# Strassen's seven products for the output matmuls of a fused attention and MLP kernel on Trainium2

## The chip, the cores and the metric

One core of a Trainium2 chip. The metric is the device time of one execution in microseconds (us), the median of several runs. The engines go by the names of the profile: PE is the matmul engine, PEld its weight loads, DVE is VectorE, ACT is ScalarE, POOL is GpSimd, SP is the engine from whose queue every transfer here is issued (SPq). DVE, ACT, POOL and SP each work through their instructions in the order in which the program has them.

## What is computed

The reference, cut to the part that the change touches:

```python
def _moe2_ref(x, w_in, g_ln, w_sg, b_sg, w_out):   # x: 8 batches x 576 x 512
    h = gelu_tanh(x @ w_in)                        # d_ff = 1024
    u, v = (h[..., :512], h[..., 512:])
    v_n = (v - mean(v)) / sqrt(var(v) + 1e-06) * g_ln
    v_s = einsum('ts,bsd->btd', w_sg, v_n) + b_sg[None, :, None]
    gated = u * v_s
    return x + gated @ w_out
```

Before it come a block-wise attention (chunks of 64) and a layer norm with a feed-forward block of width 2048; their result is the x above, called x2 in the kernel.

## The kernel before, in words

Every large matmul is done with each float32 operand split into two float16 halves, hi and lo, and three products: hi·hi, hi·lo, lo·hi. So each 128-row weight tile meets three matmuls.

The rows are 36 tiles of 128. The first part of the program (attention, the first feed-forward block) runs to about 860 us and is not touched, except for one power of two in the scaling of w_out. The second part, from line 1056, handles the rows in four groups g = 0 to 3 of nine tiles; a group is two batches of 576 rows, called halves e = 0 and e = 1 (each four and a half tiles; tile 4 of the group is shared). Per group it runs these stages, in which a name like `v_unit` is a function of the kernel:

- `prepare` / `x2_make` (line 885): gets x2 of the *next* group ready, in five pieces p = 0 to 4. A piece is loaded from DRAM into a buffer `xs` (two transfers from SP, line 903), DVE makes the sums that Strassen's method needs (lines 910 to 912, one set), ACT writes the hi half (line 927), DVE the lo half (line 936), and SP issues two transposing transfers into `xT` (line 925). There are two `xs` buffers, used in turn.
- `v_unit`, `v8_unit`: the v half of x2 @ w_in; eight tiles by Strassen's seven products (`seven`, line 1109; matmuls at line 1215), the ninth plainly (line 1240). Each product of `seven` fills one PSUM bank, and DVE or ACT takes it out; four banks serve seven products, so products 2, 3 and 4 wait until banks of products 1, 5 and 7 are empty. After it come the gelu and the layer norm (`norm`, statistics at lines 1157 and 1158).
- `u_unit`, `u8_unit`: the u half, the same way (lines 1257 and 1278).
- `s_units(g, e)`: the spatial matmul with w_sg (lines 1310 and 1311), the gate u * v_s (DVE line 1321, POOL line 1328, a rest at lines 1340 and 1346), the largest absolute value of the half (ACT line 1329, DVE line 201, then two small matmuls and lines 1358 to 1364), and the split of the gated half into float16 `gh` (ACT line 1373) and `gl` (DVE line 1376).
- `o_unit(g, i)`: the output tile i, gated @ w_out: twelve matmuls of 512 columns (line 1390), one DVE instruction that scales it and adds x2 (line 1398; `xr` is loaded at line 1393 and stored at line 1401).

The order in which these are recorded is at lines 1421 to 1452; in the groups 0 to 2 the output tiles of group g stand among the v units of group g + 1. The order in which each engine gets them is then made by a list scheduler (`Plan.run`, line 93) from the costs and priorities that each `do(...)`, `pe(...)` and `op(...)` names.

Of the kernel before, what the change touches and what calls it, by code (L numbers as in the profile page):

```python
# [132 lines left out]
def fused_kernel(ctx: ExitStack, tc, qkv, w1, w2, g1, w_in, w_out, wsgt, wsgs, g2, b_sg, out):  # L133
# [675 lines left out]
    def halve(nm, n, i, m, q, full, ck):  # L809
# [142 lines left out]
    with tc.manual_schedule():  # L952
# [118 lines left out]
        wouth, woutl = (bW["wout"][:, :, x] for x in (0, 1))  # L1071
# [217 lines left out]
        def s_units(g, e):  # L1289
# [6 lines left out]
            def unit(m):  # L1296
# [27 lines left out]
                if (g, e) == (NG - 1, 1) and m > 1:  # L1324
# [5 lines left out]
                    out=gh[:, m, 640 * e:640 * e + 512].bitcast(BF16), in_=uv, func=AF.Abs, accum_out=gm.t[:, m:m + 1]  # L1330
                ), uk, [f"g{e}{m}", gm])
# [26 lines left out]
            def cols_():  # L1358
                floor(e_, scr)
                top2(e_, inv)  # L1360
                nc.vector.tensor_scalar_mul(sg, inv, 2.0 ** 14)
# [5 lines left out]
            c = slice(576 * e, 576 * e + 576)  # L1367
            uk = [f"u{x}{m}" for m in range(4) for x in ("ax", "yb")[e]] + ["u8"] * e
            n = 1 if (g, e) == (NG - 1, 1) else 2
            for m in range(0, 4, n):  # L1370
                ms = slice(m, m + n)
                gk = [f"g{e}{m + k}" for k in range(n)]
                do("ACT", 60 + 580 * n, lambda ms=ms: nc.scalar.activation(
                    out=gh[:, ms, c], in_=uT[:, ms, c], func=AF.Copy, scale=sg
                ), uk + [f"c5_{e}"], gk, 1800)
                do("DVE", 60 + 600 * n, lambda ms=ms: nc.vector.scalar_tensor_tensor(
                    out=gl[:, ms, c], in0=uT[:, ms, c], scalar=sg, in1=gh[:, ms, c], op0=ALU.mult, op1=ALU.subtract
                ), uk + [f"c5_{e}"], gk, 1800)

        def o_unit(g, i):  # L1380
            (key, ap), = take(1)
            c = slice(i * 128, i * 128 + 128)
            t = g * GT + i
            xr = ring("xr", 4, [P, D])

            def mm(h):
                n = 6 * h
                for k in (2 * h, 2 * h + 1):
                    for x, w in ((gh, wouth), (gh, woutl), (gl, wouth)):
                        nc.tensor.matmul(ap, lhsT=x[:, k, c], rhs=w[:, k], start=(n == 0), stop=(n == 11))  # L1390
                        n += 1

            do("SP", 730, lambda: nc.sync.dma_start(out=xr.t, in_=x2d[t]), [], [xr], lat=2200)
# [4 lines left out]
            do("DVE", 730, lambda: nc.vector.scalar_tensor_tensor(  # L1398
                out=xr.t, in0=ap, scalar=col(cn), in1=xr.t, op0=ALU.mult, op1=ALU.add
            ), [key, cn], [xr], 1000)  # L1400
            do("SP", 730, lambda: nc.sync.dma_start(out=out[t], in_=xr.t), [xr], [], lat=2200)
# [23 lines left out]
        for g in range(NG):  # L1425
            u_unit(g, 0)
            later = prepare(g + 1, (0, 1))
            u_unit(g, 1)
            if g + 1 < NG:
                u8_unit(g)  # L1430
            for fn in later:
                fn()
            s_units(g, 0)
            if g + 1 == NG:
                u8_unit(g)
            for fn in prepare(g + 1, (2, 3)):
# [4 lines left out]
            if g + 1 < NG:  # L1441
                v_unit(g + 1, 0)
                for i in range(4):
                    o_unit(g, i)
                v_unit(g + 1, 2)
                for i in (5, 6, 7, 8, 4):
                    o_unit(g, i)
                v8_unit(g + 1)
            else:
                for i in (0, 1, 2, 3, 5, 6, 7, 8, 4):  # L1450
                    o_unit(g, i)
# [60 lines left out]
```

## Time and profile before

| | |
|---|---|
| median of 3 runs | 1253.74 us (1253.53 to 1254.8) |
| the profiled execution | 1251.7 us, span 1249.9 us |
| busy share of the span | PE 96%, DVE 65%, ACT 45%, POOL 39% |
| mean granted clock of PE | 0.992 |
| chain that ended last, by engine | PE 70%, DVE 14%, DMA 5%, ACT 4%, POOL 3% |

The profile comes from one execution. Its windows view gives the busy time of each engine in a stretch, its chain follows the work that ended last backwards from the end, its waits say whom an engine waited for. Line numbers in it are those of the kernel before; in the changed kernel everything in the second part stands one line lower up to line 1365, and further down after that.

### The profile page before, as it was taken

How to read it: one execution, taken by the hardware profiler on the slowest of the kernel's cores; microseconds unless marked ns; L12 is line 12 of the kernel's file. 1: busy time of each engine (PE TensorE's matmuls, PEld its weight loads, DVE VectorE, ACT ScalarE, POOL GpSimd, SP SyncE). 2: the span in 40 equal slices, each digit the busy share in tenths (PEclk: the TensorE clock that was granted, in tenths of full speed). 3: DMA queues.
4: the chain of work that ended last, by engine and by line, in shares of the span. 5: the costliest groups of instructions: out<-in, count | busy, mean ns of one | idle time of the engine just before them, and what ended most of it. 6: DMA issues, size and time to landing. Idle time of an engine off the chain costs nothing.

```text
span 1249.9 us, 27025 instructions
## 1 busy us (share of the span) xinstructions
PE 1202.5 (96%) x11412; PEld 890.9 (71%) x11412; DVE 816.2 (65%) x1520; ACT 559.4 (45%) x844; POOL 481.7 (39%) x415
## 2 busy tenths in 40 slices
PE   7899999899998999999999999998999999999998
PEld 5688644577887888888888888887557456456453
DVE  6885125987777676656656664675979559547435
ACT  6776402545665533343333334342745534534321
POOL 3562302544486554444444444342522221323220
PEclk8999999989999999999999999999999999999999
DMA  9863002256321221221322120344183283272203
GB/s 316 258 209 89 1 35 76 60 175 176 87 63 58 52 86 52 69 61 52 77 52 69 52 69 19 79 103 123 35 162 109 84 169 102 84 136 66 88 1 118
DMA packets 140377, 117.81 MB, mean 94 GB/s; under 512 B 104928, under 2 KB 113120, under 8 KB 140256
## 3 DMA queue, kind: packets, MB, share of 16 engines
q1 hardware_dynamic: 140256, 116.09, 34.3%
q8 instruction: 89, 1.46, 0.5%
q14 instruction: 32, 0.26, 0.1%
HBM read 72.02 MB, written 18.87 MB: 73 GB/s over the span
## 4 chain that ended last, share of the span: by engine, by line
PE 70%; DVE 14%; DMA 5%; ACT 4%; POOL 3%; issue 3%; SPq 0%; ACTq 0%; DVEq 0%; POOLq 0%
PE bank L639 16%; PE pair L690 9%; PE pb L1390 7%; PE pb L1310 7%; PE bank L690 6%; PE pb L1215 5%; PE bank L535 5%; PE pb L1257 5%; PE pair L556 3%; PE bank L556 2%; DVE arena L661 1%; DVE tf L599 1%; DMA xs<-x2d 1%; PE pair L294 1%; DMA straw<-in_w 1%
## 5 line engine op out<-in xcount | busy, mean ns | idle before, releaser
L639 PE MATMUL bank<-xT,w1h 128*128 128x256 f16 x1792 | 302.9, 274 | 0.4 <-DVE x L568 0.4
L690 PEld LDWEIGHTS <-arena 128*128 128x128 f16 x2352 | 228.3, 98 | 40.9 <-issue 9.4
L639 PE MATMUL bank<-xT,w1l 128*128 128x256 f16 x896 | 245.0, 273 | 0.0
L668 POOL TENSOR_TENSOR arena<-arena 128x896 f16<-128x896 f32 x69 | 132.7, 1924 | 224.4 <-ACT arena L666 224.3
L639 PEld LDWEIGHTS <-w1h 128*128 128x128 f16 x1792 | 173.6, 98 | 23.3 <-issue 1.3
L666 ACT ACTIVATE arena<-arena 128x896 f16<-128x896 f32 x112 | 106.2, 949 | 181.2 <-DVE arena L663 105.9
L661 DVE TENSOR_TENSOR arena<-arena 128x256 f32<-128x256 f32 x112 | 76.8, 686 | 102.3 <-ACT arena L654 102.2
L690 PE MATMUL pair<-w2s,arena 128*128 128x256 f16 x672 | 110.6, 274 | 7.0 <-ACT u L713 5.9
L654 ACT ACTIVATE arena<-bank 128x512 f32<-128x512 f32 x112 | 66.4, 593 | 107.2 <-PE bank L639 102.0
L690 PE MATMUL pair<-w,arena 128*128 128x256 f16 x672 | 111.2, 274 | 2.9 <-DVE arena L668 1.5
L639 PEld LDWEIGHTS <-w1l 128*128 128x128 f16 x896 | 88.0, 98 | 10.4
L690 PE MATMUL bank<-w,arena 128*128 128x256 f16 x672 | 92.4, 274 | 0.0
L1328 POOL TENSOR_TENSOR uT<-uT,vs 128x512 f32<-128x512 f32 x30 | 40.7, 1357 | 132.6 <-DVE vs L1321 123.5
L535 PE MATMUL bank<-xT,w1h 128*128 128x256 f16 x512 | 87.0, 275 | 3.0 <-DMA xT<-hl 2.8
L1310 PE MATMUL pb<-wsg,vh 128*128 128x512 f16 x288 | 88.5, 380 | 0.0
L1390 PE MATMUL pb<-wout,gh 128*128 128x512 f16 x288 | 85.7, 379 | 0.0
L718 POOL TENSOR_TENSOR x<-x,u 128x256 f32<-128x256 f32 (+1 forms) x60 | 65.2, 1116 | 46.5 <-DVE x L708 34.1
L1215 PEld LDWEIGHTS <-x2T 128*128 128x128 f16 x672 | 66.0, 99 | 16.5 <-issue 6.6
L535 PE MATMUL bank<-xT,w1l 128*128 128x256 f16 x256 | 70.4, 275 | 0.0
L668 DVE TENSOR_TENSOR arena<-arena 128x896 f16<-128x896 f32 x43 | 57.3, 1333 | 17.9 <-ACT arena L666 17.8
L535 PEld LDWEIGHTS <-w1h 128*128 128x128 f16 x512 | 49.2, 98 | 13.8 <-DMA xT<-hl 3.1
L662 DVE TENSOR_TENSOR arena<-arena 128x256 f32<-128x256 f32 x112 | 55.5, 496 | 3.8
(252 smaller groups left out, 2322.4 us busy)
## 6 DMA issues: line engine op xcount, KB each, us to landing
straw<-in_w SPq DMA_DIRECT2D x16, 1023.8 KB, 5.6
qkl<-in_qkv SPq DMA_DIRECT2D x26, 512.0 KB, 3.7
x2d<-x SPq DMA_DIRECT2D x36, 256.0 KB, 2.0
xs<-x2d SPq DMA_DIRECT2D x36, 256.0 KB, 3.3
xr<-x2d SPq DMA_DIRECT2D x36, 256.0 KB, 2.9
out<-xr SPq DMA_DIRECT2D x36, 256.0 KB, 2.8
vl<-in_qkv SPq DMA_DIRECT2D x26, 256.0 KB, 2.7
qk<-in_qkv SPq DMA_DIRECT2D x10, 512.0 KB, 6.2
```

The lines of the kernel that those rows point to most:

```text
L535: nc.tensor.matmul(acc, lhsT=w[j][:, k, fc], rhs=xT.t[:, x, k], start=(n == 0), stop=(n == 11))
L556: nc.tensor.matmul(acc[i], lhsT=h[x].t[:, c], rhs=w2t[j][:, f % 2, y], start=(f == 0 and n == 0), stop=(f == NF - 1 and n == 2),)
L639: nc.tensor.matmul(acc[:, y * 256:y * 256 + 256], lhsT=w[j][:, k, fc], rhs=xT.t[:, x, k], start=(n == 0), stop=(n == 11),)
L654: op("ACT", 600, lambda: nc.scalar.activation(out=o.t[:, 0:4].rearrange("p n t -> p (n t)"), in_=acc, func=AF.Relu, scale=0.5), rd=[kb] + ...
L661: nc.vector.tensor_tensor(out=two(6, 8), in0=two(1, 3), in1=two(0, 2), op=ALU.subtract)
L666: op("ACT", 950, lambda: nc.scalar.activation(out=h.t[:, 0], in_=o.t[:, 1:8], func=AF.Copy), rd=[o] + ar, wr=[h], prio=-100)
L668: op(lo[0], lo[1], lambda: lo[2].tensor_tensor(out=h.t[:, 1], in0=o.t[:, 1:8], in1=h.t[:, 0], op=ALU.subtract), rd=[o], wr=[h], prio=-100)
L690: nc.tensor.matmul(acc, lhsT=h.t[:, x, n], rhs=r(y), start=(first and j == 0 and m == 0), stop=(j == 7 and m == 2), skip_group_check=True,)
L718: op("POOL", ns, lambda: nc.gpsimd.tensor_tensor(out=d(), in0=d(), in1=v(), op=ALU.add), rd=u + ["q6", "q5", "q7"], wr=[x], prio=-50)
L1215: nc.tensor.matmul(ap[:, q * 256:q * 256 + 256], lhsT=xT[:, x, a, k, c], rhs=right(b, 1, k, w), start=(first and n == 0), stop=(k == 1 and ...
L1310: nc.tensor.matmul(ap, lhsT=v[:, fc], rhs=w[:, 0:512], start=(n == 0), stop=end)
L1390: nc.tensor.matmul(ap, lhsT=x[:, k, c], rhs=w[:, k], start=(n == 0), stop=(n == 11))
```

## The change

In the groups 0, 1 and 2 the eight tiles that lie in one half or the other are multiplied with w_out by Strassen's seven products, four tiles of a half at a time (`o_pairs(g, e)`); the shared tile gets a unit of its own (`o4_unit`). The last group keeps `o_unit`. To this end

- the left sides of the products are made once per half: four sums on DVE (`sums` in `s_units`, into a new buffer `gs`), and 3840 instead of 2304 columns are split into halves (`split_g`, ACT and DVE), into `gt` and `g4` in place of `gh` and `gl`;
- the right sides are made once, in group 0 (`wout_sums`, twice: ACT, DVE, four DVE subtractions, ACT, POOL);
- a half's products are taken out of PSUM by one ACT copy and six DVE instructions, with three additions on POOL;
- `split_g` of the second half is recorded behind the first half's `o_pairs`;
- the result of the absolute value on ACT goes to a buffer `jk` that nobody reads;
- to make room, the second `xs` buffer is gone; `xr` buffers hold two tiles each.

```diff
-        gh = pb.tile([P, 4, GT * P], F16, name="gh")
+        gt = pb.tile([P, 2, 7, 2, 256], F16, name="gt")
+        g4 = pb.tile([P, 2, 4, P], F16, name="g4")
+        woT = pb.tile([P, 2, 2, 4, 256], F16, name="woT")
+        jk = pb.tile([P, 512], BF16, name="jk")
-        gl = pb.tile([P, 4, GT * P], F16, name="gl")
-        x2p["xs"].append(pb.tile([P, 9, 256], F32, name="xs1"))
...
+            def sums():
+                S = gs.t
+                for o, x, y, f in (
+                    (S[:, 1], A(0, 0), A(1, 0), ALU.subtract), (A(1, 0), A(1, 0), A(1, 1), ALU.add),
+                    (S[:, 0], A(1, 1), S[:, 1], ALU.subtract), (S[:, 2], A(0, 1), S[:, 0], ALU.subtract),
+                ):
+                    nc.vector.tensor_tensor(out=o, in0=x, in1=y, op=f)
+
+            do("DVE", 2700, sums, [], uk + [gs], 1700)
...
+            parts = [
+                (1024, lambda x: D4(x, 0), lambda: U(0), uk, [f"{gk}0"]),
+                (1536, lambda x: G[:, x, 4:7].rearrange("p n k t -> p (n k t)"),
+                 lambda: gs.t.rearrange("p n k t -> p (n k t)"), [gs], [f"{gk}1"]),
+                (1024, lambda x: D4(x, 1), lambda: U(1), uk, [f"{gk}2"]),
+                (256, lambda x: g4[:, x, :, 64 * e:64 * e + 64], lambda: uT[:, :, t0:t0 + 64], vk, [f"g4{e}"]),
+            ]
...
+        def split_g(n, dst, src, rk, wk, e, sg):
+            do("ACT", 60 + n, lambda: nc.scalar.activation(
+                out=dst(0), in_=src(), func=AF.Copy, scale=sg
+            ), rk + [f"c5_{e}"], wk, 1800)
+            do("DVE", 80 + n * 27 // 25, lambda: nc.vector.scalar_tensor_tensor(
+                out=dst(1), in0=src(), scalar=sg, in1=dst(0), op0=ALU.mult, op1=ALU.subtract
+            ), rk + [f"c5_{e}"], wk, 1800)
...
+        def o_pairs(g, e):
...
+            def mm(p, n, first):
+                a, b = SIDE2[p]
+                i = 0
+                for q in range(2):
+                    for k in range(2):
+                        for x, w in TERMS:
+                            nc.tensor.matmul(
+                                ap[n][:, q], lhsT=G[:, x, a, k, q * 128:q * 128 + 128], rhs=ro(b, k, w),
+                                start=(first and i == 0), stop=(k == 1 and x == 1), skip_group_check=True,
+                            )
+                            i += 1
...
+            prod(1, 0, 0)
+            do("ACT", 680, lambda: nc.scalar.activation(out=O(), in_=ap[0], func=AF.Copy, scale=sc),
+               [key[0], f"c5_{e}"], [o1], 1000)
+            prod(6, 1, 1)
+            do("DVE", 750, lambda: nc.vector.scalar_tensor_tensor(
+                out=O(), in0=ap[1], scalar=sc, in1=O(), op0=ALU.mult, op1=ALU.add
+            ), [key[1], f"c5_{e}"], [o1], 1000)
+            for r, c in ((1, 1), (0, 1), (1, 0)):
+                do("POOL", 1520, lambda r=r, c=c: nc.gpsimd.tensor_tensor(out=C(r, c), in0=C(r, c), in1=O(), op=ALU.add),
+                   [o1], [xr[r]], 1000)
+            prod(5, 2, 2)
+            add(2, 1, 1)
+            prod(7, 3, 1)
+            add(3, 1, 1)
+            prod(2, 0, 0)
+            add(0, 0, 0)
+            prod(3, 2, 1)
+            add(2, 0, 1)
+            prod(4, 3, 2)
+            add(3, 1, 0)
...
+            if g == 0:
+                for k in range(2):
+                    wout_sums(k)
...
+            half()
             for fn in prepare(g + 1, (2, 3)):
                 fn()
-            s_units(g, 1)
+            half = s_units(g, 1)
             for fn in prepare(g + 1, (4,)):
                 fn()
...
+            v_unit(g + 1, 0)
+            o_pairs(g, 0)
+            half()
+            v_unit(g + 1, 2)
+            o_pairs(g, 1)
+            o4_unit(g)
+            v8_unit(g + 1)
```

The schedule moves with it, which the following pieces show as the program has it, without times.

First DVE in group 0, where the gate of the second half ends and the v products of the next group come out of PSUM. Before (`vt` is the rest of the spatial product, `o` and `hv` the v products, `xs` the sums for x2, `gm` and `red` the half's maximum, `xr` an output tile):

```order
L1340 SCALAR_TENSOR_TENSOR vt<-pb_10697,c_c_5173,bb 128x64 x4
L1126 SCALAR_TENSOR_TENSOR o_11526<-pb_10696,e2g,o_11526 128x512
L910 TENSOR_TENSOR xs_5485<-xs_5485 128x2x256
L911 TENSOR_TENSOR xs_5485<-xs_5485 128x2x256
L912 TENSOR_TENSOR xs_5485<-xs_5485 128x256
L1346 TENSOR_TENSOR uT<-uT,vt 128x4x64
L201 TENSOR_REDUCE gm<-uT 128x1
L1126 SCALAR_TENSOR_TENSOR hv<-pb_10697,e2g,o_11526 128x2x256
L201 TENSOR_REDUCE red<-gm 128x1
L1126 SCALAR_TENSOR_TENSOR hv<-pb_10694,e2g,hv 128x2x256
```

And in the changed kernel (`gs` are the new sums of the half, the second `o` row belongs to the output products):

```order
L1341 SCALAR_TENSOR_TENSOR vt<-pb_10697,c_c_5173,bb 128x64 x4
L1127 SCALAR_TENSOR_TENSOR o_11554<-pb_10696,e2g,o_11554 128x512
L1471 SCALAR_TENSOR_TENSOR o_11584<-pb_10692,c_c_0_10723,o_11584 128x512
L936 SCALAR_TENSOR_TENSOR hh_5486<-xs_5485,i2g,hh_10714 128x512
L1347 TENSOR_TENSOR uT<-uT,vt 128x4x64
L201 TENSOR_REDUCE gm<-uT 128x1
L1391 TENSOR_TENSOR gs<-uT 128x512
L1391 TENSOR_TENSOR uT<-uT 128x2x256
L1391 TENSOR_TENSOR gs<-uT,gs 128x512 x2
L201 TENSOR_REDUCE red<-gm 128x1
L1127 SCALAR_TENSOR_TENSOR hv<-pb_10697,e2g,o_11554 128x2x256
```

The four sums have come between the gate and the `hv` row that empties bank 10697, and one x2 piece has made place for the short one.

Second the queue of SP in group 0, where the transposes of the next group's x2 begin. Before:

```order
L903 DMA xs_5485<-x2d_84 128x2x256
L903 DMA xs_5485<-x2d_80 128x2x256
L903 DMA xs_10715<-x2d_85 128x2x256
L903 DMA xs_10715<-x2d_81 128x2x256
L925 DMA_TRANSPOSE x2T<-hh_10708 128x14x128
L925 DMA_TRANSPOSE x2T<-hh_10709 128x14x128
```

And in the changed kernel:

```order
L903 DMA xs_5485<-x2d_83 128x2x256
L903 DMA xs_5485<-x2d_79 128x2x256
L925 DMA_TRANSPOSE x2T<-hh_10711 128x14x128
L925 DMA_TRANSPOSE x2T<-hh_10712 128x14x128
L925 DMA_TRANSPOSE x2T<-hh_10713 128x14x128
L925 DMA_TRANSPOSE x2T<-hh_10714 128x14x128
L903 DMA xs_5485<-x2d_84 128x2x256
L903 DMA xs_5485<-x2d_80 128x2x256
L925 DMA_TRANSPOSE x2T<-hh_5486 128x14x128
L903 DMA xs_5485<-x2d_85 128x2x256
```

The loads of the third piece (tiles 84 and 80) and of the fourth (85 and 81) stood ahead of all transposes; now the third stands behind four of them, and the fourth further down.

## Rows read from the trace of the kernel before

**Rows 1.** Whom PE waited for, 860 to 1250 us (total, times, longest).

```profile
PE pb L1215 <- DVE hv L1126: 2.5, 1, 2.5
PE pb L1215 <- DVE x L708: 2.0, 1, 2.0
PE pb L1257 <- DVE uT L1126: 1.5, 2, 1.0
PE pb L1215 <- DVE vt L1340: 0.8, 1, 0.8
```

**Rows 2.** Busy time by stretch; the first row names the columns.

```profile
core 0: us, PE busy (x) PEld busy (x) DVE busy (x) ACT busy (x) POOL busy (x), PEclk, DMA share, GB/s
907.00:943.50 36.50, 36.22 (x289) 20.52 (x289) 27.50 (x40) 15.66 (x24) 9.06 (x8) 1.00 0.78 159
943.50:983.40 39.90, 39.90 (x246) 23.70 (x244) 35.43 (x66) 22.50 (x27) 12.11 (x12) 1.00 0.31 101
983.40:1004.00 20.60, 20.60 (x132) 10.76 (x131) 8.47 (x13) 8.15 (x11) 4.31 (x5) 1.00 0.26 74
1004.00:1038.50 34.50, 34.50 (x285) 19.77 (x283) 22.93 (x34) 14.52 (x22) 9.24 (x7) 1.00 0.82 161
1038.50:1078.60 40.10, 39.24 (x242) 23.32 (x240) 33.46 (x65) 19.69 (x26) 9.03 (x12) 1.00 0.31 99
...
1100.00:1132.50 32.50, 32.50 (x269) 18.46 (x268) 20.37 (x35) 11.43 (x22) 11.27 (x8) 1.00 0.66 121
1132.50:1172.90 40.40, 40.40 (x250) 24.13 (x249) 24.25 (x50) 18.32 (x24) 13.17 (x12) 1.00 0.28 85
```

**Rows 3.** The chain that ended last: start us, us, what, instructions.

```profile
938.30 5.24 PE pb L1215 x48
...
958.66 9.17 PE pb L1215 x84
967.83 12.95 PE pb L1390 x60
```

**Rows 4.** Groups of DVE, by form, 860 to 1250 us (busy us, mean ns, idle before).

```profile
L936 DVE SCALAR_TENSOR_TENSOR hh<-xs,i2g,hh 128x1792 f16<-128x1792 f32 x12 | 28.3, 2360 | 13.4 <-DMA x2T<-hh 11.5 <-ACT hh L927 1.9
...
L1398 DVE SCALAR_TENSOR_TENSOR xr<-pb,c_c,xr 128x512 f32<-128x512 f32 x32 | 23.7, 747 | 13.2 <-PE pb L1390 13.2
...
L912 DVE TENSOR_TENSOR xs<-xs 128x256 f32<-128x256 f32 x12 | 5.0, 416 | 0.0
...
L1325 DVE TENSOR_TENSOR uT<-uT,vs 128x512 f32<-128x512 f32 x2 | 1.4, 686 | 0.0
```

**Rows 5.** DVE in order of time, around the end of group 0's spatial stage.

```profile
939.85 2.74 DVE L1376 SCALAR_TENSOR_TENSOR gl<-uT,c_sg,gh 128x1152 f16<-128x1152 f32 x2
942.51 0.74 DVE L1321 SCALAR_TENSOR_TENSOR vs<-pb,c_c,bb 128x512 f32<-128x512 f32 x1
943.17 0.84 DVE L1340 SCALAR_TENSOR_TENSOR vt<-pb,c_c,bb 128x64 f32<-128x64 f32 x4
```

**Rows 6.** Groups of ACT and of POOL, by form, 860 to 1250 us.

```profile
L1373 ACT ACTIVATE gh<-uT,c_sg 128x1152 f16<-128x1152 f32 x14 | 16.8, 1244 | 2.5 <-DVE c_sg L1361 2.5
...
L1328 POOL TENSOR_TENSOR uT<-uT,vs 128x512 f32<-128x512 f32 x30 | 40.7, 1357 | 132.6 <-DVE vs L1321 123.5 <-DVE red L201 6.4 <-ACT hh L927 2.7
```

**Rows 7.** POOL in order of time, two places in group 0.

```profile
914.30 1.27 POOL L1328 TENSOR_TENSOR uT<-uT,vs 128x512 f32<-128x512 f32 x1 [8.62 <-DVE vs L1321]
...
966.01 2.20 POOL L1199 TENSOR_TENSOR vl<-hv,vh 128x1024 f16<-128x1024 f32 x1
```

**Rows 8.** DVE at the same two places.

```profile
914.34 3.11 DVE L936 SCALAR_TENSOR_TENSOR hh<-xs,i2g,hh 128x1792 f16<-128x1792 f32 x1
...
965.55 0.68 DVE L910 TENSOR_TENSOR xs<-xs 128x512 f32<-128x512 f32 x1
966.26 2.50 DVE L911 TENSOR_TENSOR xs<-xs 128x512 f32<-128x512 f32 x1
```

**Rows 9.** The queue of SP in order of time, group 0.

```profile
910.06 17.53 SPq L925 DMA_TRANSPOSE x2T<-hh  x8
927.65 1.99 SPq L903 DMA_DIRECT2D xs<-x2d  x3
```

**Rows 10.** The chain that ended last, at the loads of x2 in group 1.

```profile
1019.67 4.37 DMA xs<-x2d
```

More of the change, by code (lines that the diff above doesn't have):

```diff
@@ L1366, in s_units @@
             do("DVE", 700, cols_, [sk], [f"c5_{e}", "c5_m"], 2000)
[L1367 to L1378, printed above, removed]
+            if g == NG - 1:
+                c = slice(576 * e, 576 * e + 576)
+                uk = [f"u{x}{m}" for m in range(4) for x in ("ax", "yb")[e]] + ["u8"] * e
+                n = 1 + (e == 0)
+                for m in range(0, 4, n):
+                    ms = slice(m, m + n)
+                    split_g(
+                        576 * n, lambda x, ms=ms: gl4[:, x, ms, c], lambda ms=ms: uT[:, ms, c], uk,
+                        [f"g{e}{m + k}" for k in range(n)] + [k for k in xk if k[-1] != "4"] * (e == 0), e, sg
+                    )
+                return None
@@ new lines, in halves @@
+            def halves():
+                for part in parts:
+                    split_g(*part, e, sg)
+            return halves
+        def split_g(n, dst, src, rk, wk, e, sg):
[5 more added lines that the diff above has]
+            ), rk + [f"c5_{e}"], wk, 1800)
@@ new lines, in o4_unit, with mm @@
+        def o4_unit(g):
+            (key, ap), = take(1)
+            t = g * GT + 4
+            xr = ring("xr", 4, [P, 2, D])
+            load_x(t, xr, 0)
+            def mm():
+                n = 0
+                for k in range(4):
+                    for x, w in TERMS:
+                        nc.tensor.matmul(ap, lhsT=g4[:, x, k], rhs=wo[:, k, w], start=(n == 0), stop=(n == 11))
+                        n += 1
+            pe(2600, mm, ["g40", "g41"], [key])
+            do("DVE", 730, lambda: nc.vector.scalar_tensor_tensor(
+                out=xr.t[:, 0], in0=ap, scalar=col("c5_m"), in1=xr.t[:, 0], op0=ALU.mult, op1=ALU.add
+            ), [key, "c5_m"], [xr], 1000)
+            store_x(t, xr, 0)
@@ L1397, in o_unit, with wout_sums, sums @@
             cn = "c5_m" if i == 4 else f"c5_{es[0]}"
[L1398 to L1399 removed]
+            do("DVE", 750, lambda: nc.vector.scalar_tensor_tensor(
+                out=xr.t[:, 0], in0=ap, scalar=col(cn), in1=xr.t[:, 0], op0=ALU.mult, op1=ALU.add
             ), [key, cn], [xr], 1000)
[L1401 removed]
+            store_x(g * GT + i, xr, 0)
+        def wout_sums(k):
+            bf, tf = (ring("hv", 4, [P, 2, 512]) for _ in range(2))
+            w = lambda x: wo[:, k:k + 3:2, x]
+            do("ACT", 1080, lambda: nc.scalar.activation(out=bf.t, in_=w(0), func=AF.Copy), [], [bf])
+            do("DVE", 1200, lambda: nc.vector.scalar_tensor_tensor(
+                out=bf.t, in0=w(1), scalar=1.0, in1=bf.t, op0=ALU.mult, op1=ALU.add
+            ), [], [bf])
+            def sums():
+                b = bf.t.rearrange("p k (h e) -> p k h e", h=2)
+                t = tf.t.rearrange("p k (h e) -> p (k h) e", h=2)
+                for o, x, y in (
+                    (t[:, 0], b[:, 0, 1], b[:, 0, 0]), (t[:, 1], b[:, 1, 1], t[:, 0]),
+                    (t[:, 2], b[:, 1, 1], b[:, 0, 1]), (t[:, 3], b[:, 1, 0], t[:, 1]),
+                ):
+                    nc.vector.tensor_tensor(out=o, in0=x, in1=y, op=ALU.subtract)
+            flat = lambda: tf.t.rearrange("p k e -> p (k e)")
+            dst = lambda x: woT[:, k, x].rearrange("p n e -> p (n e)")
+            do("DVE", 1500, sums, [bf], [tf])
+            do("ACT", 1080, lambda: nc.scalar.activation(out=dst(0), in_=flat(), func=AF.Copy), [tf], ["woT"])
+            do("POOL", 2150, lambda: nc.gpsimd.tensor_tensor(out=dst(1), in0=flat(), in1=dst(0), op=ALU.subtract), [tf], ["woT"])
         def prepare(g, ps):
@@ L1425, in fused_kernel @@
         for g in range(NG):
+            more = g + 1 < NG
             u_unit(g, 0)
@@ L1428, in fused_kernel @@
             u_unit(g, 1)
-            if g + 1 < NG:
+            if more:
                 u8_unit(g)
+            if g == 0:
+                for k in range(2):
+                    wout_sums(k)
             for fn in later:
                 fn()
-            s_units(g, 0)
-            if g + 1 == NG:
+            half = s_units(g, 0)
+            if not more:
                 u8_unit(g)
+                s_units(g, 1)
+                for i in (0, 1, 2, 3, 5, 6, 7, 8, 4):
+                    o_unit(g, i)
+                break
+            half()
             for fn in prepare(g + 1, (2, 3)):
                 fn()
-            s_units(g, 1)
+            half = s_units(g, 1)
             for fn in prepare(g + 1, (4,)):
                 fn()
[L1441 to L1451, printed above, removed]
+            v_unit(g + 1, 0)
[5 more added lines that the diff above has]
+            v8_unit(g + 1)
         plan2.run()
```

60 lines of the change are left out of this document (49 added, 11 removed).

## The prediction

> **What bounds the kernel now.** I read the waits of PE first, then the windows, then the chain, then single groups. In the second part of the program (860 us to the end) PE hardly ever waits: four kinds of wait, 6.8 us together, all but 0.8 of them before 908 us [rows 1]. From there it is busy in every stretch at a granted clock of 1.00 [rows 2], and the chain runs through its matmuls [rows 3]. So a column less on PE is time saved, as long as DVE, ACT and POOL deliver in time. DVE is the one to look at: in group 0 it is busy 27.50 of 36.5 us in the spatial stage and 35.43 of 39.9 in the stage of the output and v products; in group 1 it is 22.93 of 34.5 and 33.46 of 40.1, in group 2 20.37 of 32.5 and 24.25 of 40.4. In between, in the u stage, it has much room (8.47 of 20.6) [rows 2].
>
> **What PE saves.** An output tile is twelve matmuls of 512 columns. Sixty of them take 12.95 us: 215.8 ns each, 2.59 us for a tile, 20.7 us for eight tiles [rows 3]. The new product has twelve matmuls of 256 columns; the v products have the same shape, and 84 of them take 9.17 us: 109.2 ns each, 1.31 us for a product [rows 3]. Fourteen products per group are 18.3 us. The saving is 2.4 us per group, 7.1 us over three groups (0.57%). A bound from below is nothing (if the shape did not hold its pace), from above there is none; I take 7.1, since the row is for the same operand types and shape.
>
> The Trainium skill, in "TensorE: Matmul & The Clock Gate" under "Back-to-back issue gap", gives about 131 ns as the sustained spacing of matmuls of 512 columns and 81 for 128 columns. By those figures (98 ns for 256 columns, an estimate between the two) eight tiles would cost 12.6 us before and 16.5 now, and the change would lose about 12 us. The trace disagrees with the rule at 215.8 ns [rows 3], so I give it no chance of its own.
>
> **What DVE gets.** Per half: four sums of 512 columns at 0.686 us [rows 4], 2.74 us. The lo halves go from 2304 to 3840 columns; 1152 columns take 1.37 us where nothing disturbs them (2.74 us for two) [rows 5], so 1536 more are 1.83 us. Six instructions take the products out of PSUM in place of four, at 0.747 us [rows 4]: 1.49 us. Together 6.1 us per half, 12.1 per group. Once, in group 0, the right sides: twice a pass of 1024 columns (1.22 us at the same rate) and four subtractions of 256 columns at 0.416 [rows 4], 5.8 us, of which the order puts half into the u stage of group 0 and half behind it.
>
> **What ACT and POOL get.** ACT: 1536 more columns per half at 1244 ns for 1152, and one copy of about 0.7 us: 2.4 us per half. It is busy 15.66 of 36.5 and 22.50 of 39.9 us [rows 2, 6], so I cost this at nothing; without that cover a half's splits would come 1.7 us later. POOL: three additions per half at 1.27 to 1.36 us [rows 6, 7], 4.0 us; it is busy 13.17 of 40.4 us at most [rows 2], so its own time is covered too. The buffer `jk`, the scaling and the larger `xr` cost nothing that the rows show: the same instructions and bytes go through the same queues.
>
> **But POOL delays DVE.** At 914.34 DVE begins its 1792-column pass just after POOL began a 1.27 us multiplication, and takes 3.11 us; the mean of that form is 2.36. At 966.26 a sum of `xs` begins inside a 2.20 us POOL instruction and takes 2.50 us, where its neighbour took 0.68 [rows 4, 7, 8]. Both read two operands from SBUF; instructions that read PSUM keep their 0.75. The new sums, the splits and the `xs` sums are all of the first kind, and POOL's three additions start right after the `o` of the output products, ahead of the gate and the sums of the second half. So each half can cost DVE up to 3 x 1.27 = 3.8 us more. "SBUF — State Buffer" in the Trainium skill ("SBUF: two separate sides") calls this an exclusive lock that one instruction holds to its end, the loser blocking fully. The trace agrees: 966.26 to 968.76 is what was left of POOL's instruction plus about one undisturbed sum.
>
> **One `xs` buffer.** The third piece's load now stands on SP behind four transposes, each 17.53 / 8 = 2.19 us of the queue [rows 9], where it stood ahead of them. I walk through group 0 with the order and these durations (estimates). DVE is done with the u products at about 908. The second half of the right sides, one lo pass and two `vs` bring it to 918. The transposes start at about 907.5, the load is issued at 916.3 and lands 4.4 us later [rows 10], at 921: DVE stands still for 3 us, with `vs` rows queued behind. The fourth piece costs another 2 us in the same way. After it come the splits of the first half (two times 1.37 us before, 4.6 now). The last `vt` ends at about 948, where it ended at 944.0 [rows 5]. PE passes this point with little wait, since the schedule has put that bank's product later. But then the order piece bites: the `hv` row that frees bank 10697 stands behind the gate and four sums. PE wants the bank at about 952 to 953. Without the lock the row is done at 954.7, with it at 957.8. Further on DVE is behind at the last output products of the pair. I get 3.3 us of PE waits in group 0 without any lock and 7.0 us with it. I take 5.9, nearer to the second, because the rows show the lock at each place where I looked.
>
> **Group 1 and 2.** The sums of two further x2 pieces move from the output stage into the idle u stage, so DVE has about 18 us of room [rows 2] for 12.1 and the lock. A walk gives 1.6 us of waits, in place of the 0.8 that stand there now [rows 1]: 0.8 more; the ends are 0 and 4. Group 2 has 28 us of room: 0.3, ends 0 and 2. In the u stage of group 0, two sets of `xs` sums and a lo pass leave and 3 us come: of the 1.5 us that PE waits there [rows 1] I let 0.5 go, ends 0 and 1.5.
>
> **The sum.** -7.1 + 5.9 + 0.8 + 0.3 - 0.5 = -0.6 us against the profiled execution's 1251.7 us: 1251.1. That execution lies 2.0 us under the median of the runs, so in medians 1253.74 - 0.6 = 1253.1 us. A measurement of this kernel can tell about 0.2% (2.5 us) from no change; the forecast lies inside.
>
> **The rivals.**
> 1. *DVE keeps up.* POOL's additions fall where DVE reads PSUM, and the waits of rows 1 after 890 us go: 3.3 us in group 0, the 0.8 of group 1 and 1.0 of the u stage gone: -7.1 + 3.3 - 0.8 - 1.0 = -5.6, 1248.1 us. For it speaks the idle time: 13.5 us of DVE in group 0 against 15 added, from which some 6 us of x2 work have moved on. Against it the standing still at the loads.
> 2. *The lock costs every half* (slower). In each of the three groups the additions of POOL meet sums and splits, 3.8 us per half at the worst, and the bank of P5 or P3 comes late both times: 7 us of waits in group 0, 4 in group 1, 2 in group 2, and none of the u stage's gone: -7.1 + 7.0 + 4 + 2 - 0.5 = +5.4, 1259.1 us. It decides against the change once PE's new waits pass 7.1 + 2.5 = 9.6 us. For it: group 1's output stage has 6.6 us of room on DVE for 7 to 8 of new work in that stage. Against it: in before PE waits 0.8 us there although DVE is already full.
> 3. *The products do not hold their pace*, because twelve weight loads per 256 columns get in the way: the saving is gone, 1260 us. The v products [rows 3] speak against it.
>
> **How the numbers follow.** The forecast has 0.41, with 1250.5 to 1256 as its own range; 0.06 of it lies beyond 0.2% on the fast side and 0.03 on the slow side. Rival 1 has 0.31, rival 2 0.26, rival 3 0.02. Faster: 0.31 + 0.06 = 0.37; slower: 0.26 + 0.02 + 0.03 = 0.31; same: 0.32. The range goes from just above the case in which all of 7.1 is kept, 1247.0, to the middle of rival 2, 1258.5, and leaves out about 0.2.
>
> **What would show it.** Right: output products at 1.31 us each; in group 0 DVE standing still at the `xs` sums for 2 to 4 us behind the transposes; one PE wait of 2 to 5 us in the v products at about 952 us, released by DVE's `hv`; new sums of 512 columns near 0.7 us where POOL is quiet and near 2 us where it is not; groups 1 and 2 shorter by 1 to 2.5 us each. Wrong: no wait of PE above 1 us in group 0 (rival 1), or waits of several us in all three groups (rival 2), or products slower than 1.35 us (rival 3).

## The result, and the profile after

The changed kernel takes 1260.75 us (median of 9 runs, 1257.14 to 1263.28), the kernel before 1253.53 us (9 runs, 1249.66 to 1257.83): a ratio of 1.0054, 95% interval 1.0036 to 1.0072. It is slower by 0.5%, and above the range of the forecast (1250.5 to 1256 us).

The profiled execution has a span of 1261.5 us, 11.6 us more than that of before; it is the slowest of the nine runs, and by the medians the change loses 7.2 us. Stage by stage, cut where PE starts the u products of a group and, in group 0, where it starts the spatial products, the kernel before reads (windows view, columns as in [rows 2]):

```profile
886.66:909.87 23.21, 21.70 (x135) 11.14 (x134) 22.11 (x37) 18.29 (x22) 13.06 (x10) 1.00 0.15 47
909.87:983.21 73.34, 73.34 (x521) 42.95 (x520) 60.20 (x100) 36.19 (x49) 20.98 (x19) 1.00 0.56 134
983.21:1078.45 95.24, 94.38 (x653) 53.85 (x652) 64.87 (x111) 42.22 (x59) 22.61 (x24) 1.00 0.48 117
1078.45:1172.69 94.24, 94.24 (x654) 53.75 (x652) 53.08 (x97) 38.81 (x57) 30.19 (x25) 1.00 0.43 96
```

and the changed kernel, with three short stretches of group 0 below the dots:

```profile
889.83:918.29 28.46, 24.48 (x136) 12.11 (x135) 27.36 (x41) 19.02 (x23) 13.38 (x11) 0.88 0.12 31
918.29:999.03 80.74, 74.36 (x595) 51.33 (x593) 68.94 (x113) 35.11 (x50) 29.92 (x25) 0.96 0.43 94
999.03:1091.09 92.06, 91.83 (x726) 60.77 (x724) 76.12 (x129) 45.45 (x63) 33.94 (x30) 1.00 0.49 127
1091.09:1183.57 92.48, 91.84 (x727) 60.82 (x725) 71.38 (x123) 45.43 (x65) 33.65 (x28) 1.00 0.48 113
...
910.09:915.16 5.07, 5.07 (x13) 1.72 (x13) 4.77 (x5) 2.74 (x4) 2.13 (x1) 0.50 0.00 0
964.27:966.91 2.64, 2.64 (x12) 1.62 (x11) 1.45 (x3) 0.00 (x0) 0.00 (x0) 0.50 0.00 0
994.92:997.44 2.52, 2.52 (x13) 1.72 (x13) 2.49 (x5) 0.00 (x0) 0.00 (x0) 0.50 0.27 104
```

The u products of group 0 start 3.2 us later (889.83 against 886.66), and the v products ahead of them already did (864.42 against 860.96), after code that the change does not touch; that belongs to the execution. Group 0 takes 12.65 us more: 5.25 in its u stage (28.46 for 23.21) and 7.40 from there to the next u stage. Group 1 is 3.2 us shorter, group 2 is 1.8 us shorter, and the rest, from the u products of group 3 to the end, is 0.7 us longer (77.93 for 77.21). So the new products gain about what they should in two groups of three, and group 0 loses it all and more. The three stretches at the bottom show something that [rows 2] have nowhere: a granted clock of 0.50, that is 1.2 GHz.

PE's waits (answers to [rows 1]) and the places in group 0 in PE's order of time:

```profile
PE pb L206 <- DVE red L201: 4.3, 3, 3.5
PE pb L1258 <- DVE uT L1127: 4.0, 2, 3.5
PE pb L1453 <- DVE xr L1463: 2.5, 1, 2.5
PE pb L1216 <- DVE hv L1127: 2.5, 2, 2.2
```

```profile
910.09 2.72 PE L1258 MATMUL pb<-x2T,win 128*128 128x512 f16 x6 [3.51 <-DVE uT L1127]
...
963.61 0.38 PE L206 MATMUL pb<-ident,red 128*1 128x128 f32 x2 [3.49 <-DVE red L201]
964.27 2.72 PE L1216 MATMUL pb<-win,x2T 128*128 128x256 f16 x12 [0.28 <-DVE hv L1127]
...
973.95 1.47 PE L1453 MATMUL pb<-woT,gt 128*128 128x256 f16 x12
975.26 1.47 PE L1216 MATMUL pb<-winT,x2T 128*128 128x256 f16 x12
...
994.92 2.72 PE L1453 MATMUL pb<-wout,gt 128*128 128x256 f16 x12 [2.53 <-DVE xr L1463]
```

Three waits on DVE, of 3.51, 3.49 and 2.53 us, and behind each of them PE works at half clock: twelve matmuls of 512 columns take 5.07 us (910.09 to 915.16) in place of 12 x 215.8 ns = 2.59, a product of twelve 256-column matmuls 2.64 and 2.52 us in place of 1.31 [rows 3]. With what is left of the slow stretches behind them (0.45 and 0.28 us) the clock costs 2.48 + 0.45 + 1.33 + 1.21 + 0.28 = 5.75 us. The Trainium skill says in "TensorE: Matmul & The Clock Gate" ("HAM oscillation — how this bites in real kernels") that a PE which waits between pieces of work falls to half clock and starts the next piece slowly; this trace agrees at these three places, but not behind a wait of 2.24 us in the v stage (the last section has it).

Why DVE was late at the first of them (DVE, and the POOL row of the same time):

```profile
901.53 3.61 DVE L936 SCALAR_TENSOR_TENSOR hh<-xs,i2g,hh 128x1792 f16<-128x1792 f32 x1
905.07 0.74 DVE L1127 SCALAR_TENSOR_TENSOR o<-pb,e2g,o 128x512 f32<-128x512 f32 x1
905.73 3.65 DVE L1546 TENSOR_TENSOR hv<-hv 128x256 f32<-128x256 f32 x4
909.29 0.74 DVE L1127 SCALAR_TENSOR_TENSOR uT<-pb,e2g,o 128x512 f32<-128x512 f32 x1
```

```profile
901.13 7.29 POOL L1200 TENSOR_TENSOR vl<-hv,vh 128x1024 f16<-128x1024 f32 x3 [0.37 <-ACT vh L1199]
```

The four subtractions for w_out's right sides stand ahead of the `uT` row that PE needs, and POOL's `vl` work stretches them, and the x2 pass ahead of them, to 3.65 and 3.61 us (1.55 for the four at 919.19 and 2.08 for the pass at 917.20). At the second place:

```profile
958.12 1.30 DVE L1391 TENSOR_TENSOR gs<-uT 128x512 f32<-128x512 f32 x1
959.52 1.57 DVE L1391 TENSOR_TENSOR uT<-uT 128x512 f32<-128x512 f32 x1
961.02 2.47 DVE L1391 TENSOR_TENSOR gs<-uT,gs 128x512 f32<-128x512 f32 x2
963.40 0.15 DVE L201 TENSOR_REDUCE red<-gm 128x1 f32<-128x5 f32 x1
```

```profile
956.83 5.38 POOL L1475 TENSOR_TENSOR xr<-xr,o 128x512 f32<-128x512 f32 x3 [0.81 <-DVE o L1471]
```

The maximum `red` stands behind the four sums, and these run beside POOL's three additions: 5.3 us in place of 2.74. PE's queue holds the small transpose of `red` (L206) ahead of the v products, so all of PE waits. And the reason that DVE comes to this point late, SP and DVE earlier in the group:

```profile
915.39 8.82 SPq L925 DMA_TRANSPOSE x2T<-hh  x4
924.31 1.68 SPq L903 DMA_DIRECT2D xs<-x2d  x2
```

```profile
928.83 0.69 DVE L910 TENSOR_TENSOR xs<-xs 128x512 f32<-128x512 f32 x1 [2.76 <-DMA xs<-x2d]
```

The third piece's loads stand behind four transposes, and DVE stands still for 2.76 us.

At the third place, the wait on `xr`, the `xs` sums of a later piece stand ahead of the output rows, beside POOL's next three additions, which its `vl` work follows at once (988.95, 3.87 us):

```profile
986.33 1.53 DVE L910 TENSOR_TENSOR xs<-xs 128x512 f32<-128x512 f32 x1
987.90 1.64 DVE L911 TENSOR_TENSOR xs<-xs 128x512 f32<-128x512 f32 x1
989.46 2.34 DVE L912 TENSOR_TENSOR xs<-xs 128x256 f32<-128x256 f32 x1
```

```profile
984.81 4.18 POOL L1475 TENSOR_TENSOR xr<-xr,o 128x512 f32<-128x512 f32 x3 [0.62 <-DVE nb L1171]
```

The three take 5.4 us (986.33 to 991.73), where three such sums took 1.7 at the third piece (928.83 to 930.50).

### The profile page after: what moved, and what is told of

Its sections match the earlier page's. It is cut to its first block, busy times and chain, and to the rows that moved or that the text cites. A ratio compares the mean times of both kernels' runs of the same rounds, so it can differ in the third digit from the quotient of the medians.

```text
span 1261.5 us, 27575 instructions
## 1 busy us (share of the span) xinstructions
PE 1203.1 (95%) x11628; PEld 915.1 (73%) x11628; DVE 860.8 (68%) x1578; ACT 575.4 (46%) x866; POOL 511.3 (41%) x435
## 4 chain that ended last, share of the span: by engine, by line
PE 67%; DVE 15%; DMA 5%; ACT 4%; POOL 3%; SPq 2%; issue 2%; DVEq 0%; ACTq 0%; POOLq 0%
PE bank L639 17%; PE pair L690 9%; PE bank L690 7%; PE pb L1216 5%; PE bank L535 5%; PE pb L1258 5%; PE pb L1453 4%; PE pb L1311 4%; PE pair L556 3%; PE bank L556 2%; SPq L925 2%; DMA xs<-x2d 2%; DVE arena L661 1%; DMA straw<-in_w 1%; PE pair L294 1%
## 5 line engine op out<-in xcount | busy, mean ns | idle before, releaser
L690 PE MATMUL bank<-w,arena 128*128 128x256 f16 x672 | 92.5, 274 | 0.0
L1329 POOL TENSOR_TENSOR uT<-uT,vs 128x512 f32<-128x512 f32 x30 | 43.3, 1448 | 106.1 <-DVE vs L1322 106.1
L1453 PEld LDWEIGHTS <-gt 128*128 128x128 f16 x504 | 49.9, 99 | 10.4 <-issue 3.1
```

Of the source, the lines that this page charges most:

```text
L690: nc.tensor.matmul(acc, lhsT=h.t[:, x, n], rhs=r(y), start=(first and j == 0 and m == 0), stop=(j == 7 and m == 2), skip_group_check=True,)
L1453: nc.tensor.matmul(ap[n][:, q], lhsT=G[:, x, a, k, q * 128:q * 128 + 128], rhs=ro(b, k, w), start=(first and i == 0), stop=(k == 1 and x = ...
```

## The experiments

Each was timed beside the kernel before in the same series; the ratios are to that. "The change" has 1260.75 us and stages of 28.5, 80.7, 92.1 and 92.5 us (u stage of group 0, rest of group 0, group 1, group 2).

### e1_sums_early and e2_max_before_sums: the two late places, one by one

```diff
         v_unit(0, 0)
+        for k in range(2):
+            wout_sums(k)
         v_unit(0, 2)
...
-            if g == 0:
-                for k in range(2):
-                    wout_sums(k)
```

> The sums of w_out's right sides are recorded behind the first v unit of group 0 (with uT's still empty rows as scratch), not behind the u products. Theory W (they broke the u stage: 5.3 us there, 3.5 of them a wait of PE, the rest at half clock): the u stage of group 0 takes 23 to 24 us again instead of 28.5, PE's wait on uT falls from 3.5 to under 1 us, and the time falls by 4 to 6 us, to about 1255.5. Rival D (VectorE is full in group 0, so work that is moved only moves the wait): the 5 us come back as waits in the v stage or behind, and the time stays within 1.5 us of 1260.5. Rival X (the single xs buffer does it all): no change in the waits behind the u stage, u stage 26 us or more, time 1259 or more.

1258.29 us, ratio 1.0037 (1.0023 to 1.0051). The u stage came down to 21.6 us, below before's 23.2 and below the 23 to 24 of theory W; but the v stage ahead of it went from 25.4 to 29.9. ScalarE's two copies of w_out could start only behind the stores of x2, at 869.05, and the first `o` copy of the v products stood behind them; PE waited 3.1 us for that. The place was diagnosed rightly, but the new place was better by only 2.5 us, which lies between theory W and rival D.

e2 takes the four sums apart and records them behind the row maximum:

```diff
             do("DVE", 260, lambda: rowmax(scr), [sk], ["rowm"], 2000, lat=500)
+                for o, x, y, f in (...):
+                    do("DVE", 690, lambda o=o, x=x, y=y, f=f: nc.vector.tensor_tensor(out=o(), in0=x(), in1=y(), op=f),
+                       ["rowm"], uk + [gs], 1700)
...
-            do("DVE", 2700, sums, [], uk + [gs], 1700)
```

> The four sums of u's halves are recorded behind the row maximum and as four instructions that the planner may part, where they stood as one block ahead of the column maximum. Theory S (the block of sums delays the small transpose in the second half of group 0: 3.5 us of wait and 1.3 at half clock): that wait goes, the time falls by 3 to 5 us, to about 1256.5. Rival D (VectorE is full in group 0): PE waits as long, on something else behind it; the time within 1.5 us of 1260.5. Rival X (the single xs buffer): the same time as under D, with VectorE's idle time at the xs loads unchanged at 3 us or more.

1250.16 us, ratio 0.9977 (0.9963 to 0.9992): 10.6 us less than the change, twice what theory S gave. Its windows for group 0:

```profile
885.29:912.38 27.09, 23.11 (x136) 11.45 (x135) 26.45 (x41) 18.38 (x22) 13.39 (x11) 0.94 0.11 30
912.38:983.33 70.95, 70.95 (x595) 49.92 (x593) 61.97 (x109) 32.66 (x48) 27.41 (x24) 1.00 0.50 116
```

From the spatial products on PE does not wait at all: 70.95 us, all busy, 2.4 under before's 73.34, which is the saving of the products and nothing else. With the wait on `red` gone, the later one on `xr` and the slow clock behind both went too; the wait of 3.5 us on `uT` in the u stage stays. VectorE is busy 61.97 of these 70.95 us, so rival D falls there; and it still idles 3.48 us at an `xs` load (923.64), so that idling alone costs PE nothing.

### e3_groups_1_2 and e4_before_one_xs: the products and the buffer apart

```diff
-            if g == NG - 1:
+            if g == NG - 1 or g == 0:
...
-            if g == 0:
+            if g == 1:
...
                 for k in range(2):
                     wout_sums(k)
```

> Seven products in groups 1 and 2 only: group 0 makes its output tiles as before, and the right sides are summed in the u stage of group 1. Still one xs buffer. Theory (all that was lost was lost in group 0, 12.7 us, while groups 1 and 2 gained 3.2 and 1.8): group 0 is within 3 us of before's 96.6, the u stage of group 1 hides the right sides, and the time is 1248 to 1251, faster than before by 2.5 to 5 us. Rival X (one xs buffer is what costs): group 0 keeps 5 us or more of the loss, time 1255 to 1258. Rival E (the right sides break whichever u stage they stand in): group 1 longer by 5 us than in the change, 1254 to 1256.

1252.07 us, ratio 0.9988 (0.9977 to 0.9999). Groups 1 and 2 take 93.4 and 91.8 us, with the right sides hidden in the u stage of group 1. But group 0, which now does what it did before, takes 100.1 us in place of 96.6: neither theory's number, and the time, too, lies between the forecasts. e4 has the single buffer alone, and there group 0 loses about as much.

```diff
-        x2p["xs"].append(pb.tile([P, 9, 256], F32, name="xs1"))
```

> The kernel before with one xs buffer in place of two, and nothing else of the change. My theory (the buffer makes VectorE stand still for 3 to 5 us in group 0, where before has 13.5 us of room): 1253.5 to 1256, under 2.5 us slower than before. Rival X (the buffer alone is the loss): 1258 to 1262. Rival: the load order gets better for the queue and the time falls by 1 to 2 us.

1259.88 us, ratio 1.0048 (1.0032 to 1.0064). My number was wrong and rival X right: without any of the new products, one buffer in place of two costs 6.2 us: 3.9, 1.6 and 0.7 in the groups 0, 1 and 2.

### e5_both, e6_one_block_behind, e12_four_in_place: other ways to the same end

```diff
                 pe(1720, lambda: mm(1), vk, [key, tk])
+                if (g, e) == (0, 0) and m < 2:
+                    wout_sums(m, [key])
```

> The edit of e2 and, beside it, the right sides' sums recorded in the spatial stage of group 0, each set behind one spatial unit, so that the u stage holds none of them. Theory (u stage 27.1 us in e2 against 21.8 where it holds no right sides; from there on e2 runs at PE's own pace): the u stage takes 21.5 to 23 us, the rest of group 0 stays within 1.5 us of 71.0, and the time is 1244 to 1247. Rival D (VectorE is full in group 0): the sums come back as waits of 3 us or more in the spatial stage, time 1249 to 1251.

1262.79 us, ratio 1.0073 (1.0051 to 1.0095), far above both forecasts. The u stage is right (21.85 us), but now one wait of 4.8 us on `vt` stands in the spatial stage of group 0, whose rest takes 77.9; and the planner's new order has PE waiting 4.8 us on `uT` and 4.1 on other rows in later stages.

e6 has the block of e2's place, unparted; e12 has the four parts in the old place (`["rowm"]` in the code above is `[]`, and the rows stand where `sums` stood).

> As e2, but the four sums stay one block of the planner's: only their place is changed, to behind the row maximum. Theory order (what cost was that the maximum, for which PE's queue waits, stood behind the block): 1250 to 1252, the wait on red under 0.5 us. Rival granularity (the gain of e2 is that the planner can part the four): 1255 to 1258, with a new wait of 2 us or more on the scale columns' small matmul or on hv.

> The change with the four sums as four of the planner's operations, recorded where the block was, ahead of the maximum. Theory (order and size of the pieces both matter, since the small transpose then waits for one sum and not for four): the wait on red falls from 3.5 to 1 us or less, time 1252 to 1257. Rival (a new order puts VectorE late elsewhere, as it did in e6): 1259 to 1265, with waits of 2 us or more on uT or xr.

e6: 1265.20 us, 1.0092 (1.0075 to 1.0109). e12: 1261.78 us, 1.0071 (1.0053 to 1.0088). In both the wait on `red` is under 0.8 us, and group 0 is down to 101.1 and 98.8 us. But groups 1 and 2 rise to 100.1 and 97.4 in e6, 97.3 and 97.5 in e12, with waits on `uT`, `xr`, `vt` and others of up to 1.9 us each. So e6 falls out of both forecasts, and e12 met the time of its rival's. An edit in one place lets the planner set other rows elsewhere; which of those rows costs what in groups 1 and 2 was not tried and stays open.

### e7_dummies_in_waits and e10_e2_with_dummies: the clock

```diff
+        def dummy(t, n):
+            for _ in range(n):
+                nc.tensor.matmul(t, lhsT=xT8[:, 0, 0], rhs=win[:, 0, 0, 0:512], start=True, stop=True)
...
```

> The change with 15, 15 and 10 extra matmuls of 512 columns, whose results nothing reads, put into PE's queue ahead of the three matmuls that waited 3.5, 3.5 and 2.5 us in group 0; every other instruction on every engine as in the change. Theory C (after such a wait PE goes at a granted clock of 0.50 for 2.7 to 5.1 us, which costs 5 to 6 us in all): the next products take 1.31 us and 2.6 us per 12 matmuls, not 2.6 and 5.1, and the time falls by 4 to 5.5 us, to about 1256. Rival L (the slow matmuls come from something else, such as the weight loads or the bank): they stay as slow and the time rises by 0 to 1 us.

1256.24 us, ratio 1.0020 (1.0006 to 1.0034): 4.5 us less than the change, with PE doing more. The first two places (L1105 is the dummy):

```profile
906.58 3.40 PE L1105 MATMUL pb<-win,x2T 128*128 128x512 f16 x15
910.27 1.46 PE L1266 MATMUL pb<-x2T,win 128*128 128x512 f16 x6 [0.28 <-DVE uT L1135]
...
961.11 0.38 PE L206 MATMUL pb<-ident,red 128*1 128x128 f32 x2 [0.26 <-DVE red L201]
961.76 1.47 PE L1224 MATMUL pb<-win,x2T 128*128 128x256 f16 x12 [0.28 <-DVE hv L1135]
```

The data comes no earlier (0.28 us are left of the 3.51), but what follows runs at full clock: the two windows of group 0 are 25.4 and 78.1 us, together 5.7 us shorter, the 5.75 counted above. Rival L falls.

> e2 with 15 extra matmuls of 512 columns, whose results nothing reads, in PE's queue ahead of the u product that waits 3.5 us in group 0; all else as in e2. Theory C (clock): the product behind the wait takes 2.6 us for 12 matmuls instead of 4.2, nothing else changes, time 1.5 to 2.5 us lower than e2, about 1248. Rival (the wait itself is all): within 0.7 us of e2's 1250.2.

1248.83 us, ratio 0.9970 (0.9957 to 0.9983); the u stage goes from 27.1 to 25.5 us and nothing else moves. The medians of e10 and e2 are 1.3 us apart, a little under the forecast, and their two series cannot tell that from nothing; the stage shows 1.56.

### e8_no_o_additions: POOL

```diff
-                do("POOL", 1520, lambda r=r, c=c: nc.gpsimd.tensor_tensor(out=C(r, c), in0=C(r, c), in1=O(), op=ALU.add),
+                do("POOL", 1520, lambda: None,
                    [o1], [xr[r]], 1000)
```

> The change without POOL's three additions of the shared partial o to xr per half, which leaves those parts out of the output; every other instruction keeps its place. Theory P (these additions hold VectorE off and stretch the second half's sums from 2.7 to 5.3 us): the sums take 2.8 us, the wait on red falls from 3.5 to about 1 us, and the time falls by 2.5 to 5 us, to about 1257. Rival order (the block of sums is in the way whether stretched or not): under 1.5 us.

1251.90 us, ratio 0.9987 (0.9968 to 1.0006), 8.9 us less than the change, more than theory P gave. The sums on DVE at the place shown above:

```profile
956.90 0.68 DVE L1391 TENSOR_TENSOR gs<-uT 128x512 f32<-128x512 f32 x1
957.68 0.69 DVE L1391 TENSOR_TENSOR uT<-uT 128x512 f32<-128x512 f32 x1
958.29 1.41 DVE L1391 TENSOR_TENSOR gs<-uT,gs 128x512 f32<-128x512 f32 x2
```

2.7 us in place of 5.3, with every row in its place. The wait on `red` falls to 0.9 us, and the one on `xr` is gone: the `xs` sums ahead of it take 2.0 us (981.13 to 983.15) in place of 5.4. The rest of group 0 is 72.6 us in place of 80.7. "SBUF — State Buffer" in the Trainium skill ("SBUF: two separate sides") has a DVE instruction with two SBUF inputs and a POOL instruction that reads SBUF take turns, each held to its end; this run agrees.

### e11_change_two_xs and e13_two_xs_old_order: what the single buffer costs

```diff
-        woT = pb.tile([P, 2, 2, 4, 256], F16, name="woT")
+        x2p["xs"].append(pb.tile([P, 9, 256], F32, name="xs1"))
...
-            return woT[:, k, x, n - 4]
+            return wo[:, n // 2 % 2 * 2 + k, x, n % 2 * 256:n % 2 * 256 + 256]
```

> The change with its second xs buffer given back. For the room, the sums of w_out's right sides are made as before but written where group 0's gt comes later, and the products that would read them read other blocks of w_out of the same size, so those parts of the output are not what they should be; the count and shapes of all instructions stay. Theory X (the single buffer costs here what it costs in the kernel before, 6 us, by late loads that make VectorE late): 1253 to 1256. Rival P (the POOL additions and the block of sums are what costs, with two buffers too): 1258.5 to 1261.

1249.98 us, ratio 0.9972 (0.9959 to 0.9984): the whole loss is gone, 10.8 us, more than theory X gave. Group 0 takes 93.7 us (22.6 and 71.1), groups 1 and 2 95.5 and 92.9. POOL's additions, the block of sums and the right sides are all still there, the first set of right sides still in the u stage. For room `vt` has one buffer in place of two, here and in e13.

e13 has both buffers too, but the planner sees one:

```diff
-        b = Buf(f"{tag}{k}", None)
+        b = Buf(tag + "0" if tag == "xs" else f"{tag}{k}", None)
```

> As e11 (two xs buffers, and the same parts of the output are not what they should be), but the planner is told of one buffer, so every engine and SP's queue keep the order of the change; only the loads and sums use the two buffers in turn. Theory Q (what the single buffer costs is the place that it gives to the loads in the queues, behind the transposes, and to the sums on VectorE behind them): VectorE stands still for 2.5 to 3.5 us at the same loads, time 1258.5 to 1261.5. Rival H (it is the wait for the buffer itself): about e11's 1250.0, under 1252.5. In between (1253 to 1258) both have a part.

1261.14 us, ratio 1.0058 (1.0044 to 1.0072): the change's time. Stages 28.4, 80.8, 92.3 and 92.4 us, waits on `red`, `uT` and `xr` of 3.5, 3.5 and 2.5 us as in the change. In e13 the second buffer lets the second piece's loads go out at 871.08 (905.17 in the change), and it buys nothing; the third piece's still stand behind four transposes (921.60). In e11 the third piece's loads go out at 904.02, ahead of all transposes, which begin at 907.45. DVE at the third piece in e13, then in e11:

```profile
926.14 0.69 DVE L910 TENSOR_TENSOR xs<-xs 128x512 f32<-128x512 f32 x1 [3.52 <-DMA xs<-x2d]
```

```profile
907.90 0.69 DVE L910 TENSOR_TENSOR xs<-xs 128x512 f32<-128x512 f32 x1 [0.86 <-DMA xs<-x2d]
```

So nothing waited for the buffer as such. What costs is the order in every queue that the planner makes when it believes that there is one buffer. Theory Q holds, rival H falls. Which rows of that order cost what was not tried one by one.

### e9_sums_behind_u and e14_second_set_later: a version that beats both

e9 is e2 with the right sides' subtractions held back until `uT` is out of PSUM:

```diff
-            do("DVE", 1500, sums, [bf], [tf])
+            do("DVE", 1500, sums, [bf] + ["ub1", "ub3"], [tf])
```

> e2 with the four subtractions of each set of right sides held back until the u products have been taken out of PSUM; two places in VectorE's order change, PE's and SP's order stay as in e2. Theory (in e2 the first set stands ahead of a uT row for which PE waits 3.5 us, and then goes at half clock): the u stage takes 21.8 to 23.5 us instead of 27.1, the rest of group 0 stays within 1 us of 70.95, and the time falls to 1244.5 to 1247. Rival D (VectorE is full): the wait comes back behind it, 1249 to 1251.

1247.84 us, ratio 0.9960 (0.9946 to 0.9974), between the two forecasts. Its windows for group 0:

```profile
887.22:909.36 22.14, 21.54 (x135) 11.10 (x134) 19.86 (x35) 14.99 (x19) 11.10 (x10) 1.00 0.14 36
909.36:982.75 73.39, 71.23 (x595) 50.04 (x593) 70.37 (x115) 36.11 (x51) 31.16 (x25) 1.00 0.50 112
```

The u stage is 5 us shorter, at full clock; 2.2 us of it come back as waits on `vt` and `red` in a stretch where DVE is now busy 70.4 of 73.4 us.

> e9 with the second set of right sides behind the second spatial unit's evacuation; one row of VectorE's order moves, two each of ScalarE's and GpSimd's, PE's order stays. Theory (in e9 that set makes the evacuation late and PE waits 1.2 and 1.0 us): these waits go, the rest of group 0 takes 71.0 to 71.8 us in place of 73.4, time 1245.5 to 1247.5. Rival D (VectorE has no room there, the wait goes elsewhere): 1247.5 to 1249.

1246.95 us, ratio 0.9951 (0.9934 to 0.9967). The stages are e9's to 0.05 us, and 2.2 us of waits are still there (1.8 on `vt`, 0.4 on `red`), so the reading of the trace is rival D's: DVE has no room there. The 0.9 us between the two medians is less than the series can tell. Both keep one `xs` buffer and are 0.4 to 0.5% faster than the kernel before, 1% faster than the change.

## Why the prediction was wrong, point by point

**Right: what the products save.** 1.31 us per product (973.95 to 975.26 for the twelve shown above); groups 1 and 2 gain 3.2 and 1.8 us where the sum had 1.6 and 2.1, and e2's group 0, without waits, gains the 2.4. Rival 3 falls.

**Right, but under-used: the lock and the late loads.** DVE stands still at the third piece for 2.76 us (forecast 3) and at the fourth for 0.88 (forecast 2). The third came at 928.8 in place of 921: 3.2 us of that are the execution's, the rest is about what the u stage lost. New sums take 0.68 us alone and 1.3 to 1.6 beside POOL. The 5.9 us of PE waits in group 0's spatial and output stages measured 6.3 (3.49 + 0.28 + 2.53). Their place was off: I expected the row behind the sums that would hold PE up to be `hv`, at 952 to 953 us; the wait ended at 963.6, and the row was `red`, which stands directly before `hv` in the order shown and which PE wants earlier in its queue, through the small transpose.

**Wrong: no term for the clock.** The sum took a wait for as long as it lasts. Behind each of the three waits PE ran at 1.2 GHz, which cost 5.75 us more, 2.93 of them in the u stage; e7's two windows lost just that. From 907 us on the trace of before has no long wait and so no such stretch. But the forecast put waits of 2 to 5 us on a PE that [rows 2] show at 1.00 throughout, and gave no bound for what follows such a wait. The trace of before has one, ahead of where [rows 2] begin:

```profile
860.96 1.50 PE L1215 MATMUL pb<-win,x2T 128*128 128x256 f16 x12 [1.95 <-DVE x L708]
862.26 5.76 PE L1215 MATMUL pb<-winT,x2T 128*128 128x256 f16 x36
...
873.17 1.47 PE L1215 MATMUL pb<-winT,x2T 128*128 128x256 f16 x12 [2.53 <-DVE hv L1126]
```

Soon after the wait of 1.95 us the 36 matmuls took 5.60 us (862.26 to 867.86) in place of 3.93, at a granted clock of 0.50 until 865; behind the wait of 2.53 us the twelve took 1.31, at 1.00. A price from nothing to 1.7 us a wait stood there to be read, if not yet the 2.93 of the u stage.

**Wrong: "in the u stage of group 0 ... I let 0.5 go".** It came out at +5.25: PE waited 2.5 us more there (3.97 for 1.51) and lost 2.9 to the clock. I counted the rows that left the stage and the 3 us that came, and asked how much of its waits would go, never where the rows stand: the subtractions stand ahead of a `uT` row, beside 7.3 us of POOL. DVE was busy 22.1 of 23.2 us there before; the table in [rows 2] starts at 907 and leaves that stretch out. e9, which moves them, brings the stage to 22.1 us.

**Wrong: the buffer as a wait.** I priced the single buffer by how long DVE would stand still. e2 shows that such idling can be free, e4 that the buffer costs 6.2 us without any new product, e11 and e13 that it costs 10.8 us here, and through the order alone. Two pieces of that order were shown ahead of the prediction, but I costed only the standing still and the late `hv`.

The sum had +3.0 us for group 0 (-2.4 + 5.9 - 0.5). With these in place group 0 is -2.4 (products) + 6.3 (waits) + 2.8 (their clock) + 5.25 (u stage) = 12.0 of the 12.65 measured; the rest of 0.7 is not assigned. Rival 2 was near in time (1259.1), but it is not what happened: groups 1 and 2 have 0.2 and 0.6 us of waits, not 4 and 2. There DVE keeps up, as rival 1 had it for all three.

The causes don't add up, since they are one chain: e2, e8 and e11 each take off 9 to 11 us of a loss of 7. DVE late by a few us, a block of sums ahead of a maximum for which PE's queue waits, POOL stretching that block, and the clock behind it. Breaking one link let the saving of the products through in these three; e6 and e12 broke the link at `red`, too, and lost the gain in groups 1 and 2, where the planner's new order has DVE late elsewhere.

## What to carry to other kernels

A wait that moves onto PE's queue costs its length and can cost a slow stretch behind it; here 9.5 us of waits cost 5.75 more. Before a buffer is given up, compare the whole order that the planner makes with one and with two, since the price lay in the order and not in the buffer. And record a reduction whose result the matmul queue needs ahead of bulk work on the same engine, with the bulk work in pieces; then look at the new order as a whole, since e2 did both and gained 10.6 us, while e6 and e12, with one of the two each, gained nothing.

## What was not expected of the hardware

Matmuls whose results nothing reads shortened the kernel: forty of them, 8.6 us of PE work at 215.8 ns, in the waits, took 4.5 us off. And not every wait drops the clock: behind a wait of 2.24 us in the v stage (876.35) twelve 256-column matmuls took 1.30 us, full speed, while behind 2.53 us at 994.92 they took 2.52. The length of the wait alone does not decide it: in the kernel before, twelve such matmuls behind a wait of 2.53 us (873.17) ran at full speed. What else does was not tried.
